# One chunk pipeline before a long loop: ScalarE's evictions run ahead of VectorE's, key rows lag by a row block, one scale for all values, last recalls in four banks

## The chip, the core and the metric

The kernel runs on one NeuronCore of a Trainium2 chip. The number compared is the device time of one execution in microseconds (us). The kernel before the change takes 1706.84 us, the median of 3 runs that lie between 1706.77 and 1707.49 us. The profile is one more execution, taken with the hardware profiler on.

The engines are named as the profile does it: PE (TensorE, with its weight loads as PEld), DVE (VectorE), ACT (ScalarE), POOL (GpSimd) and SP (SyncE, which issues the DMAs). Each engine takes its instructions in the order of its own list, and waits at an instruction until what it needs is there.

## What is computed

The input x has 2048 rows (tokens) of 576 columns. Two results of it are mixed, row by row, with a gate:

```python
g = sigmoid((x * gate_w).sum(-1))
out = g * A(x) + (1 - g) * B(x)
B = (gelu(x @ w_gate) * (x @ w_up)) @ w_down          # hidden width 4608
# A: 32 heads of 18, four chunks of 512 tokens, one after the other
for s in range(4):
    q, k, v = the rows of chunk s of x @ wq, x @ wk, x @ wv
    a_dot = softmax(q k^T * 18**-0.5 + causal mask) @ v
    a_mem = phi(q) M / (phi(q) z + 1e-6)               # "recall"
    o[s]  = sigmoid(beta) * a_mem + (1 - sigmoid(beta)) * a_dot
    M, z  = M + phi(k)^T v, z + sum(phi(k))            # "memorize"
A = o @ wo
phi(t) = t + 1 if t > 0 else exp(t)
```

The weights come in float32. Products with x are made in pairs of fp16 words (a high word and the rest, the low word), scaled by powers of two that are taken from sums of squares.

## The kernel before

The program has three parts. Lines 569 to 761 (the code in the `manual_schedule(engines=ORDERED)` block) project x to queries, keys and values and carry the memory along; this text calls them the opening. Then 72 steps of a loop compute the attention of the 32 heads, for two halves of the tokens, beside the feed-forward B; an end multiplies by wo. Nearly all of the span is the loop, and the change is in the opening and at the loop's first steps.

**The opening's stages.** For a chunk s of 512 tokens there are two stages. In the *rows* of chunk s (s = 1, 2, 3) four row blocks q of 128 tokens follow each other: `vrows(s, q, 0)` and `vrows(s, q, 1)` make the two halves of the value rows (14 matmuls each, in banks `dn`, L312 to L315), `key_rows(s-1, q)` turns the phi of the earlier chunk's keys by five transposes (L531 to L534), `recall` multiplies the phi of its queries with the memory (12 matmuls, L508; from chunk 1 on) and `memorize` adds its keys and values to the memory (L546, banks `U` and `pv`). In the *products* of chunk s come nine chains `project(s, j)` of 14 matmuls of 512 columns (L302 to L305): j = 0 to 4 hold the queries, 4 to 8 the keys. Chain j goes to PSUM bank `G` (j % 4 = 0), `U` (1) or one of two `st`. For chunk 0 the value rows are made first, from float32 words, while the weights arrive, and only the products belong to the stage as said. The recalls of the last chunk come after its chains 5 to 8.

**Evicting a chain** takes: on ACT the high word to the tile `stage` (L449), and where phi is wanted a Relu (L453) and an Exp (L454); on DVE the linear half of phi (L455) and the low word (L457); on POOL the sum of both halves (L456); then a DMA of `stage` to DRAM (L458). `stage` has two buffers. These are written directly behind the chain that they evict.

**Beside the chains.** In the stages of the opening other work is fitted in by `beside_rows` and `beside_products`: pairs of words of the weights (`make_qk`, `make_v`, L103 on ACT and L104 on DVE), the next chunk of x (`next_x`: load, squares, scale, high words on ACT L160, low words on DVE L165), sums of two chunks of x that the feed-forward uses (`load_sums` and `load_rest` L329 and L335, `form_sums`: L349 on DVE, L350 on ACT, L352 on DVE), and in chunk 3 the weights of the first two blocks of the feed-forward (`squares` L80, `scale_g` L252, `sums_g` L272 to L275, `high_g` L279, `low_g` L283). `keep_memory` (L559, L560) moves the memory from PSUM to the tile `bd`, which the next recalls read.

**What sets the order.** In the opening and the loop PE, ACT, DVE and POOL keep the order in which the program is written. SP's order is set by a scheduler, which places each DMA by when it expects the data and the buffer.

## Time and profile before

| what | value |
|---|---|
| median of 3 runs | 1706.84 us |
| the profiled execution | 1714.4 us, its span 1712.7 us |
| mean clock granted to PE | 0.988 |
| PE busy in the span | 1645.0 us (96%) |
| chunk 0's chains to the end of the last chain of chunk 3 (31.72 to 275.48) | 243.76 us |
| the loop and the end (275.48 to 1712.70) | 1437.22 us, PE busy 1406.47 us |

In rows of a timeline the first number is when an instruction (or a row of equal ones, x12) starts, in us from the span's start, and the second how long it takes; then engine, line, operation, output tile <- input tiles, shape. `[1.72 <-DVE stage L457]` behind it says that the engine was idle for 1.72 us before, and that what it waited for ended with VectorE's line 457. Rows of windows give the busy time of each engine in a stretch of the span and the granted clock (1.00 is full).

### The profile page before, as it was taken

To read this page: it belongs to the slowest core of one execution; us is meant where nothing else is said; L and a number is where in the kernel's file an instruction comes from. 1 tells how busy PE (TensorE), PEld (TensorE's weight loads), DVE (VectorE), ACT (ScalarE), POOL (GpSimd) and SP (SyncE) were. 2 spreads that over 40 slices of the span, in tenths; PEclk is the share of its full clock that TensorE was granted. 3 is DMA by queue.
4 is the path that set the end of the run, shared out by engine and by line. 5 is a ranking of instruction groups with operands and counts; after the bars stand their busy time and mean duration, and the time that the engine had idled before them with its cause. 6 is when DMAs were issued, how large, how long until landed. Compare 5 with 4: busy or idle time off the path is not lost.

```text
span 1712.7 us, 31984 instructions
## 1 busy us (share of the span) xinstructions
PE 1645.0 (96%) x11886; PEld 989.7 (58%) x11886; DVE 1267.3 (74%) x3169; ACT 1081.7 (63%) x1768; POOL 1162.8 (68%) x1070
## 2 busy tenths in 40 slices
PE   8899869799999999999999999999999999999999
PEld 4456544355655565555655565555555565565577
DVE  5556566588888878888887778788887888876553
ACT  6565341677777776777677777777777777762200
POOL 3331371888888787888878687978878697876300
PEclk9999888999999999999999999999999999999999
DMA  6532323357565656647465656547465655534441
GB/s 205 200 101 93 112 84 101 72 107 130 109 123 114 126 125 118 128 100 138 102 133 112 134 123 117 124 107 137 107 129 112 141 123 112 120 78 114 92 118 63
DMA packets 462348, 200.54 MB, mean 117 GB/s; under 512 B 421232, under 2 KB 431728, under 8 KB 461680
## 3 DMA queue, kind: packets, MB, share of 16 engines
q1 hardware_dynamic: 462192, 198.50, 52.0%
q8 instruction: 93, 1.52, 0.4%
q14 instruction: 63, 0.52, 0.1%
HBM read 82.60 MB, written 27.26 MB: 64 GB/s over the span
## 4 chain that ended last, share of the span: by engine, by line
PE 67%; DVE 16%; ACT 6%; POOL 6%; issue 3%; DMA 2%; DVEq 0%; ACTq 0%; SPq 0%; POOLq 0%
PE dn L908 17%; PE U L950 13%; PE V L950 7%; PE G L950 7%; PE pv L862 3%; PE st L312 3%; DVE pf L820 3%; PE st L814 2%; DVE acc L916 2%; PE V L957 2%; DVE junk L80 2%; PE dn L312 2%; POOL hh L935 2%; PE U L957 2%; PE G L957 1%
## 5 line engine op out<-in xcount | busy, mean ns | idle before, releaser
L908 PE MATMUL dn<-paird,hh 128*128 128x288 f16 x3402 | 488.6, 286 | 5.1 <-DVE acc L916 4.1
L950 PEld LDWEIGHTS <-pairg 128*128 128x128 f16 x3024 | 290.9, 98 | 300.5 <-issue 30.6
L843 POOL TENSOR_TENSOR ph<-pf,ph 128x512 f16<-128x512 f32 (+1 forms) x256 | 359.1, 1403 | 97.9 <-ACT ph L842 61.0
L908 PEld LDWEIGHTS <-hh 128*128 128x128 f16 x3456 | 337.2, 98 | 144.4 <-issue 8.3
L916 DVE SCALAR_TENSOR_TENSOR acc<-dn,ev,acc 128x288 f32<-128x288 f32 x535 | 268.1, 512 | 51.3 <-PE dn L908 48.9
L833 ACT ACTIVATE pf<-pf,mb,esc 128x512 f32<-128x512 f32 (+3 forms) x512 | 293.0, 642 | 3.0
L935 POOL TENSOR_TENSOR hh<-gl,hh 128x512 f16<-128x512 f32 x144 | 173.0, 1201 | 178.9 <-ACT hh L934 178.9
L820 DVE CUSTOM_DVE_ANT_0 pf<-st,mask 128x512 f32<-128x512 f32 (+3 forms) x512 | 229.2, 485 | 76.0 <-PE st L814 72.8
L950 PE MATMUL U<-xt,pairg 128*128 128x512 f16 x864 | 211.0, 380 | 4.8 <-DVE gl L1064 3.9
L950 PE MATMUL G<-x,pairg 128*128 128x512 f16 x864 | 210.7, 380 | 0.0
L283 POOL TENSOR_TENSOR pairg<-raw,pairg 128x512 f16<-128x512 f32 (+2 forms) x144 | 180.9, 1279 | 13.8 <-ACT pairg L279 13.8
L842 ACT ACTIVATE ph<-pf 128x512 f16<-128x512 f32 (+1 forms) x256 | 184.3, 720 | 0.0
L940 ACT ACTIVATE gl<-gl,sc 128x512 f32<-128x512 f32 x144 | 103.6, 720 | 98.3 <-DVE gl L1081 54.1
L830 ACT ACTIVATE mb<-mx,esc 128x4 f32<-128x4 f32 x128 | 37.3, 292 | 192.2 <-DVE mx L820 192.1
L934 ACT ACTIVATE hh<-gl 128x512 f16<-128x512 f32 x144 | 89.6, 622 | 85.3 <-DVE gl L930 85.3
L252 POOL TENSOR_SCALAR raw<-raw,sc 128x640 f32<-128x640 f32 x72 | 138.8, 1940 | 0.0
L1064 DVE COPY gl<-U 128x512 f32<-128x512 f32 x72 | 49.8, 692 | 108.9 <-POOL hh L935 55.3
L950 PE MATMUL V<-x,pairg 128*128 128x512 f16 x432 | 105.7, 381 | 11.4 <-DVE gl L1049 11.4
L814 PE MATMUL st<-kt,qt 72*128 72x512 f16 (+3 forms) x512 | 111.5, 299 | 0.6 <-DVE mx L820 0.6
L950 PE MATMUL U<-x,pairg 128*128 128x512 f16 x432 | 105.5, 380 | 2.5 <-DVE gl L1081 2.3
L950 PE MATMUL V<-xt,pairg 128*128 128x512 f16 x432 | 105.6, 381 | 1.5 <-DVE mo L522 1.5
L957 PEld LDWEIGHTS <-pairg 128*128 128x128 f16 x576 | 56.6, 98 | 68.6 <-issue 1.1
(247 smaller groups left out, 2590.8 us busy)
## 6 DMA issues: line engine op xcount, KB each, us to landing
raw<-in_wgu_dram SPq DMA_DIRECT2D x36, 640.0 KB
rawd<-in_wd_dram SPq DMA_DIRECT2D x36, 288.0 KB
qk<-stage SPq DMA_DIRECT2D x36, 256.0 KB
qt<-qk SPq DMA_DIRECT2D x128, 72.0 KB
kt<-qk SPq DMA_DIRECT2D x128, 72.0 KB
vp<-vstage SPq DMA_DIRECT2D x16, 296.0 KB
vt<-vp SPq DMA_DIRECT2D x16, 296.0 KB
orow<-oa SPq DMA_DIRECT2D x16, 288.0 KB
```

Source lines behind the costliest of these rows:

```text
L252: pool.tensor_scalar(r, r, scl[f // 2][0][:, 0:1], None, OP.mult)
L283: pool.tensor_tensor(spot(f, *p, 1), raw_g[f][:, p[0] : p[1]], spot(f, *p, 0), OP.subtract)
L814: pe.matmul(o[:, off : off + n], q[:, e * L + qi * P : e * L + (qi + 1) * P], kt[:, e * L : e * L + n], start=True, stop=True)
L820: dve.tensor_tensor_reduce(prob[a][:, COL[qi] : COL[qi + 1]], o[:, off : off + n], mask[:, L - n :], 1.0, -3e38, OP.add, OP.max, mx[a][:, ...
L833: act.activation(r, r, AF.Exp, bias=b[:, qi : qi + 1], scale=esc[:, 0, c : c + 1])
L842: act.activation(h[:, 0, cols], p[:, cols], AF.Copy)
L843: pool.tensor_tensor(h[:, 1, cols], p[:, cols], h[:, 0, cols], OP.subtract)
L908: pe.matmul(o[:, :NH], hh[:, a, q * P : (q + 1) * P], w[:, b, n * NH : (n + 1) * NH], start=i == 0, stop=i == 5)
L916: dve.scalar_tensor_tensor(av, o[:, :NH], ev, av, OP.mult, OP.add)
L935: pool.tensor_tensor(hh[:, 1], t, hh[:, 0], OP.subtract)
L950: pe.matmul(o, w[:, i, (a + k) * P : (a + k + 1) * P], x[:, b + k], start=start and k == 0 and i == 0 and b == h, stop=k == 1 and i == 1, ...
L957: pe.matmul(o, w[:, i, a * P : (a + 1) * P], x[:, b], start=False, stop=i == 1, skip_group_check=True)
```

## The change

1. `project` issues the matmuls alone. ACT's part of an eviction is in `put_columns(j)`, called after the matmuls of chain j+1; what DVE, POOL and SP do for it is put in a list `later` and issued by `finish_later` behind it. `put_rows` and `recall` put VectorE's part in the same list. Bank `U` is that of j % 4 = 3 now, and `key_rows` uses a bank `st` instead of `G`.
2. `key_rows` and `memorize` follow one row block behind the value rows; block 3's key rows come ahead of the chains and its memorize after chain 0. `keep_memory` comes at chain 1.
3. The value weights have one scale instead of one for each half: one `scale_v`, and five `make_v` of 578 columns instead of ten of 288 or 290. Chunk 0's opening is reordered to match.
4. The squares of chunk 1 of x go from POOL to ACT. `form_sums` of the last two chunks is one chain later.
5. In chunk 3 the scaling, sums and words of the feed-forward's block 1 are no longer among the products: they are issued as the loop's other blocks are, in its first steps.
6. The last recalls: blocks 0 and 1 after chain 6 in four banks (`dn`, `dn`, `V`, `pv`), block 2 after chain 7, block 3 at the end.

```diff
...
     def square_x(c, k):
-        r, sq = x_raw[c][k // 2][:, (k % 2) * L : (k % 2 + 1) * L], x_sq[c][:, k * L : (k + 1) * L]
-        if c == 1:
-            pool.tensor_tensor(sq, r, r, OP.mult)
-        else:
-            act.activation(sq, r, AF.Square)
+        act.activation(x_sq[c][:, k * L : (k + 1) * L], x_raw[c][k // 2][:, (k % 2) * L : (k % 2 + 1) * L], AF.Square)
     def scale_x(c):
...
-        def make_v(b, k):
-            if b == 0:
-                W[9 + k] = pa.tile([P, 2, KT * P], F16, name="wv", bufs=5)
-            pair_of(W[9 + k][:, :, VB[b]], raw_v[:, k, VB[b]], wsc[:, 1 + b : 2 + b])
+            square_sum(wst[:, 10 + j : 11 + j], raw_qk[:, j], j % 2 or j == 8)
+        def scale_v():
+            scale_sum(1, wst[:, 0 : 2 * KT])
...
+        def make_v(k):
+            t = W[9 + k] = pa.tile([P, 2, D + 2], F16, name="wv", bufs=5)
+            pair_of(t, raw_v[:, k], wsc[:, 1:2])
...
             pair_of(W[j], raw_qk[:, j], wsc[:, 0:1])
+        later = []
+        def finish_later():
+            while later:
+                later.pop(0)()
         def project(s, j):
-            hf, c = divmod(s, 2)
             w = W[j]
             i = j % 4
-            pr = bank("G") if i == 0 else bank("U") if i == 1 else bank("st", 2)
+            pr = bank("G") if i == 0 else bank("U") if i == 3 else bank("st", 2)
             chain_w(pr, lambda k, a: w[:, a, k * P : (k + 1) * P], x16[s])
+            return s, j, pr
+        def put_columns(s, j, pr):
+            hf, c = divmod(s, 2)
             st = pp.tile([P, 2, L], F16, name="stage", bufs=2)
             act.activation(st[:, 0], pr, AF.Copy, scale=2.0**-14)
-            if (j <= 4 and s >= 1) or (j >= 4 and s <= 2):
+            with_phi = (j <= 4 and s >= 1) or (j >= 4 and s <= 2)
+            if with_phi:
...
                 act.activation(e, e, AF.Exp, scale=-1.0)
-                dve.tensor_scalar(f, pr, al[:, s, 0:1], 0.0, OP.mult, OP.max)
-                pool.tensor_tensor(f, f, e, OP.add)
-            dve.scalar_tensor_tensor(st[:, 1], pr, 2.0**-14, st[:, 0], OP.mult, OP.subtract)
-            sp.dma_start(qks[hf][:, j * P : (j + 1) * P, c * L : (c + 1) * L].rearrange("a p t -> p a t"), st)
+            def rest():
+                if with_phi:
+                    dve.tensor_scalar(f, pr, al[:, s, 0:1], 0.0, OP.mult, OP.max)
+                    pool.tensor_tensor(f, f, e, OP.add)
+                dve.scalar_tensor_tensor(st[:, 1], pr, 2.0**-14, st[:, 0], OP.mult, OP.subtract)
+                sp.dma_start(qks[hf][:, j * P : (j + 1) * P, c * L : (c + 1) * L].rearrange("a p t -> p a t"), st)
+            later.append(rest)
         def put_rows(s, q, b, pv, unit, a):
...
-            put_rows(s, q, b, pv, 2.0**-14, al[:, s, 1 + b : 2 + b])
+            return pv, 2.0**-14, al[:, s, 1:2]
         def first_words(pvs, b, k, qs):
...
-            hf, c = divmod(s, 2)
-            t = 4 * c + q
-            na, nb = (spare(), spare()) if s == 3 else (bank("st", 2), bank("st", 2))
+        def recall(s, q, banks=(("st", 2), ("st", 2))):
...
                               start=first, stop=last, skip_group_check=True)
+            later.append(lambda: put_recall(s, q, na, nb))
...
         def key_rows(s, q):
-            ka, kb = bank("G"), bank("V")
+            ka, kb = bank("st", 2), bank("V")
...
-                if j == 1 + d:
-                    for k in range(3 + 2 * d):
+                if j in (2, 3):
+                    for k in ((0, 1, 2), (3, 4))[j - 2]:
                         square_x(c, k)
...
-                if j == 4 + d:
+                if j == 4:
                     scale_x(c)
...
                 if s == 2:
+                    if q:
+                        form_sums(0, q - 1, 1)
...
                     if q == 1:
-                        squares(0, 0, 0)
-                        squares(0, 0, 1)
+                        for f, i in ((0, 0), (0, 1), (1, 0), (1, 1)):
+                            squares(0, f, i)
                     if q == 2:
-                        squares(0, 1, 0)
-                        squares(0, 1, 1)
...
             def beside_products(s, j):
-                if s < 3:
-                    next_x(s + 1, j)
...
                         make_qk(j + 2)
-                    for i in ((0, 1), (2, 3, 4), (5, 6, 7), (8, 9))[j] if j < 4 else ():
-                        make_v(i // KT, i % KT)
+                    if j < 5:
+                        make_v(j)
+                if s < 3:
+                    next_x(s + 1, j)
                 if s == 2:
+                    if j == 0:
+                        form_sums(0, 3, 1)
+                        last_sum(0, 0)
+                    if j == 1:
+                        last_sum(0, 1)
...
                 if s == 3:
-                    if j in (0, 3):
-                        high_g(j // 3, 0)
-                        low_g(j // 3, 0)
-                        sums_g(j // 3)
-                    if j in (1, 4):
-                        high_g(j // 3, 1)
-                        low_g(j // 3, 1)
+                    if j == 0:
+                        high_g(0, 0)
+                        low_g(0, 0)
+                    if j == 1:
+                        sums_g(0)
                     if j == 2:
+                        high_g(0, 1)
+                    if j == 3:
+                        low_g(0, 1)
+                    if j == 4:
                         load_g(3)
-                        scale_g(1)
+                    if 3 <= j < 7:
+                        form_sums(1, j - 3, 1)
                     if 2 <= j < 6:
-                        form_sums(1, j - 2, 1)
-                    if 1 <= j < 5:
-                        form_sums(1, j - 1, 0)
-                    if j in (5, 6):
-                        squares(1, 2, j - 5)
-                    if j == 6:
+                        form_sums(1, j - 2, 0)
+                    if j in (6, 7):
+                        squares(1, 2, j - 6)
+                    if j == 7:
                         last_sum(1, 0)
+            done = None
...
                     for q in range(4):
-                        vrows(s, q, 0)
-                        key_rows(p, q)
+                        pv = vrows(s, q, 0)
+                        if done:
+                            put_columns(*done)
+                            done = None
+                        finish_later()
+                        put_rows(s, q, 0, *pv)
+                        if q:
+                            key_rows(p, q - 1)
+                        beside_rows(s, q)
+                        finish_later()
                         if p >= 1:
                             recall(p, q)
-                        beside_rows(s, q)
-                        vrows(s, q, 1)
-                        memorize(p, q)
-                        if s == 2:
-                            form_sums(0, q, 1)
-                    if s == 2:
-                        last_sum(0, 0)
-                        last_sum(0, 1)
-                    keep_memory(p)
-                make_gate(s)
...
                 for j in range(9):
+                    if j == 1:
+                        make_gate(s)
+                    pr = project(s, j)
+                    if s and j == 0:
+                        memorize(p, 3)
+                    if done:
+                        put_columns(*done)
+                    done = pr
+                    if s and j == 1:
+                        keep_memory(p)
+                    if s == 3 and j == 1:
...
-                    project(s, j)
-                    if s == 3 and j >= 5:
-                        recall(3, j - 5)
+                    finish_later()
+                    if s == 3 and j == 6:
+                        recall(3, 0, (("dn", 2), ("dn", 2)))
+                        recall(3, 1, (("V",), ("pv",)))
+                    if s == 3 and j == 7:
+                        recall(3, 2, (("dn", 2), ("dn", 2)))
+            recall(3, 3)
+            put_columns(*done)
+            finish_later()
...
         def weights_first(fb, i4):
             n0 = 2 * fb
-            if not fb and i4 < 2:
-                return
...
             if i4 == 1:
...
         def weights_high(fb, i4):
             n0 = 2 * fb
-            if fb or i4 >= 2:
-                high_g(n0 + 1 + i4 // 2, i4 % 2)
+            high_g(n0 + 1 + i4 // 2, i4 % 2)
...
             n0 = 2 * fb
-            if fb or i4 >= 2:
-                low_g(n0 + 1 + i4 // 2, i4 % 2)
+            low_g(n0 + 1 + i4 // 2, i4 % 2)
             if i4 >= 2:
                 low_d(n0 + i4 - 2)
```

What the lists of the engines look like where the prediction speaks of them:

ScalarE, the first products of chunk 3, before: `stage` and `expm` evict a chain, `xt` is the high word of a sum of two chunks, `raw` to `pairg` a weight's high word.

```order
L449 ACTIVATE stage<-G 128x512
L453 ACTIVATE expm<-G,nal 128x512
L454 ACTIVATE expm<-expm 128x512
L279 ACTIVATE pairg<-raw 128x512 x2
L350 ACTIVATE xt_2101<-acc,xsc 128x1024
L449 ACTIVATE stage<-U 128x512
L453 ACTIVATE expm<-U,nal 128x512
L454 ACTIVATE expm<-expm 128x512
L350 ACTIVATE xt_2101<-acc,xsc 128x1024
L449 ACTIVATE stage<-st 128x512
L453 ACTIVATE expm<-st,nal 128x512
L454 ACTIVATE expm<-expm 128x512
```

And now:

```order
L453 ACTIVATE stage<-G 128x512
L458 ACTIVATE expm<-G,nal 128x512
L459 ACTIVATE expm<-expm 128x512
L453 ACTIVATE stage<-st 128x512
L458 ACTIVATE expm<-st,nal 128x512
L459 ACTIVATE expm<-expm 128x512
L274 ACTIVATE pairg<-raw 128x512 x2
L345 ACTIVATE xt_2112<-acc,xsc 128x1024
L453 ACTIVATE stage<-st 128x512
L458 ACTIVATE expm<-st,nal 128x512
L459 ACTIVATE expm<-expm 128x512
L345 ACTIVATE xt_2112<-acc,xsc 128x1024
```

Two chains are evicted ahead of the first `xt` now instead of one, and the third eviction stands behind one `xt`, where it stood behind two.

VectorE at the same place, before (`acc` is a sum of two chunks, `xt` with three operands its low word):

```order
L349 TENSOR_TENSOR acc<-acc 128x1024
L455 TENSOR_SCALAR phi<-U,al 128x512
L457 SCALAR_TENSOR_TENSOR stage<-U,stage 128x512
L352 SCALAR_TENSOR_TENSOR xt_2101<-acc,xsc,xt_2101 128x1024
L349 TENSOR_TENSOR acc<-acc 128x1024
L455 TENSOR_SCALAR phi<-st,al 128x512
L457 SCALAR_TENSOR_TENSOR stage<-st,stage 128x512
L352 SCALAR_TENSOR_TENSOR xt_2101<-acc,xsc,xt_2101 128x1024
L349 TENSOR_TENSOR acc<-acc 128x1024
L455 TENSOR_SCALAR phi<-st,al 128x512
```

And now:

```order
L344 TENSOR_TENSOR acc<-acc 128x1024
L463 TENSOR_SCALAR phi<-st,al 128x512
L465 SCALAR_TENSOR_TENSOR stage<-st,stage 128x512
L347 SCALAR_TENSOR_TENSOR xt_2112<-acc,xsc,xt_2112 128x1024
L344 TENSOR_TENSOR acc<-acc 128x1024
L463 TENSOR_SCALAR phi<-st,al 128x512
L465 SCALAR_TENSOR_TENSOR stage<-st,stage 128x512
L347 SCALAR_TENSOR_TENSOR xt_2112<-acc,xsc,xt_2112 128x1024
L344 TENSOR_TENSOR acc<-acc 128x1024
L463 TENSOR_SCALAR phi<-U,al 128x512
```

VectorE's list is the same there but for the banks: `U` is the fourth chain's now.

SyncE in the products of chunk 0, before: `qk` is the store of an evicted chain, `acc` a load of the chunks of x that are summed later (2048 words for each partition, 1 MB; `2x512`, half of that).

```order
L458 DMA qk<-stage 128x2x512
L329 DMA acc<-in_xs_dram 128x2048
L458 DMA qk<-stage 128x2x512
L335 DMA acc<-in_xs_dram 128x2x512
L458 DMA qk<-stage 128x2x512
L329 DMA acc<-in_xs_dram 128x2048
L458 DMA qk<-stage 128x2x512
L329 DMA acc<-in_xs_dram 128x2048
L458 DMA qk<-stage 128x2x512 x2
L329 DMA acc<-in_xs_dram 128x2048
L458 DMA qk<-stage 128x2x512
```

And now:

```order
L324 DMA acc<-in_xs_dram 128x2048
L466 DMA qk<-stage 128x2x512
L330 DMA acc<-in_xs_dram 128x2x512
L466 DMA qk<-stage 128x2x512 x2
L324 DMA acc<-in_xs_dram 128x2048
L466 DMA qk<-stage 128x2x512
L324 DMA acc<-in_xs_dram 128x2048
L466 DMA qk<-stage 128x2x512
L324 DMA acc<-in_xs_dram 128x2048
L466 DMA qk<-stage 128x2x512
```

The loads of x's sums stood behind the first, second, third, fourth and sixth store; now they stand ahead of the first, second, fourth, fifth and sixth.

More of the change, by code (lines that the diff above doesn't have):

```diff
@@ L114, in outscale @@
         else:
[L115 to L116 removed]
+            pool.tensor_scalar(gha[:, c], gh[:, 1], al[:, c, o], 2.0**14, OP.mult, OP.mult)
     x_raw = {}
@@ L475, in put_rows, with rest @@
                 act.activation(v32[s, q][:, hs, 0:DH], p3, AF.Copy, scale=a)
-            dve.scalar_tensor_tensor(st[:, hs, DH : 2 * DH], p3, unit, st[:, hs, 0:DH], OP.mult, OP.subtract)
-            if b:
-                dve.tensor_scalar(gate[:, 0, 8 * hf + t : 8 * hf + t + 1], pv[:, NH : NH + 1], a, None, OP.mult)
-                sp.dma_start(vps[hf][t * P : (t + 1) * P, :], flat(st))
+            def rest():
+                dve.scalar_tensor_tensor(st[:, hs, DH : 2 * DH], p3, unit, st[:, hs, 0:DH], OP.mult, OP.subtract)
+                if b:
+                    dve.tensor_scalar(gate[:, 0, 8 * hf + t : 8 * hf + t + 1], pv[:, NH : NH + 1], a, None, OP.mult)
+                    sp.dma_start(vps[hf][t * P : (t + 1) * P, :], flat(st))
+            later.append(rest)
         def vrows(s, q, b):
@@ L493, in first_words @@
                           start=k == 0, stop=k == 4)
-        def recall(s, q):
-            hf, c = divmod(s, 2)
-            t = 4 * c + q
-            na, nb = (spare(), spare()) if s == 3 else (bank("st", 2), bank("st", 2))
+        def recall(s, q, banks=(("st", 2), ("st", 2))):
+            na, nb = (bank(*i) for i in banks)
             for j, (a, w) in enumerate(SPANS):
@@ L582 @@
             va = [bank("dn", 2), bank("dn", 2), bank("V"), bank("pv")]
-            for k in range(3):
+            for k in range(2):
                 first_words(va, 0, k, range(4))
@@ L1139, in finish @@
                     wos[k] = op_.tile([P, 2, D], F16, name="wo", bufs=5)
-                    pair_of(wos[k], rows[k], wsc[:, 3:4])
+                    pair_of(wos[k], rows[k], wsc[:, 2:3])
         LAG = 2
```

109 lines of the change are left out of this document (51 added, 58 removed).

## The prediction

> **What bounds the kernel now.** I read the strip of 40 slices first, for where PE is not full.
>
> ```profile
> PE   8899869799999999999999999999999999999999
> ```
>
> After slice 7 (some 300 us) PE is full to the end, so what the change can win lies ahead of that. The next view is the table of windows, cut at the stages of the opening: the products of chunk 0, then rows and products of chunks 1, 2 and 3.
>
> ```profile
> core 0: us, PE busy (x) PEld busy (x) DVE busy (x) ACT busy (x) POOL busy (x), PEclk, DMA share, GB/s
> 31.72:65.43 33.71, 29.42 (x131) 12.32 (x132) 27.32 (x48) 21.90 (x41) 14.25 (x15) 1.00 0.70 226
> 65.43:93.82 28.39, 24.66 (x173) 18.34 (x171) 11.00 (x23) 12.22 (x30) 7.64 (x18) 0.94 0.36 128
> 93.82:122.11 28.29, 28.29 (x134) 12.81 (x132) 16.86 (x33) 19.71 (x33) 12.71 (x15) 1.00 0.31 99
> 122.11:153.53 31.42, 29.65 (x221) 23.73 (x220) 19.43 (x44) 13.80 (x30) 6.40 (x12) 1.00 0.29 103
> 153.53:182.74 29.21, 28.44 (x133) 12.80 (x132) 20.41 (x38) 21.52 (x36) 12.70 (x15) 1.00 0.37 118
> 182.74:222.75 40.01, 34.83 (x224) 27.33 (x222) 18.66 (x59) 8.08 (x21) 8.21 (x13) 0.87 0.26 96
> 222.75:275.48 52.73, 37.89 (x175) 19.75 (x175) 37.01 (x61) 21.90 (x34) 34.08 (x24) 0.84 0.31 106
> ```
>
> The products of chunk 1 are the measure: nine chains and a norm's sum in 28.29 us, PE busy all of it at clock 1.00. Chunk 3 runs as much work and its four recalls, and takes 40.01 + 52.73 = 92.74 us at clocks 0.87 and 0.84. PE's timeline prices the work at full clock and shows the waits.
>
> ```profile
> 126.64 1.76 PE L508 MATMUL st<-bd,phi 128*128 128x152 f32 x12
> 133.99 1.76 PE L508 MATMUL st<-bd,phi 128*128 128x152 f32 x12
> 264.51 2.76 PE L302 MATMUL st<-x,wp 128*128 128x512 f16 x12
> 267.54 1.76 PE L508 MATMUL dn<-bd,phi 128*128 128x152 f32 x12
> 186.34 0.24 PE L531 MATMUL G<-ident,phi 64*128 64x64 f32 x1 [1.72 <-DVE stage L457]
> 187.25 3.05 PE L508 MATMUL st<-bd,phi 128*128 128x152 f32 x12
> 210.38 0.36 PE L85 MATMUL dn<-stat,ones 128*128 128x8 f32 x2 [3.43 <-DVE stat L80]
> 251.94 0.88 PE L508 MATMUL dn<-bd,phi 128*128 128x152 f32 x2 [8.89 <-POOL phi L456]
> 256.52 0.70 PE L508 MATMUL dn<-bd,phi 64*128 64x76 f32 x2 [3.71 <-POOL phi L456]
> 275.48 2.08 PE L950 MATMUL V<-xt,pairg 128*128 128x512 f16 x6 [1.46 <-DVE mo L522]
> ```
>
> From recall to recall a row block of chunk 2 takes 133.99 - 126.64 = 7.35 us; a chain takes 267.54 - 264.51 = 3.03 us; a recall 1.7. Chunk 3 at these prices: 4 x 7.35 + 0.2 (a small sum) + 9 x 3.03 + 4 x 1.7 = 63.7 us. It loses 92.74 - 63.7 = 29 us. The waits quoted at 186.34, 210.38, 251.94 and 256.52 are 17.8 us of it (the last row's, 1.46, comes after the cut); most of the rest, some 11 us, is work at a low clock behind them: the recall at 187.25 takes 3.05 us where that at 126.64 takes 1.76.
>
> **Why the recall waits 8.89 us.** It wants phi of chains 2 to 4, and these come late on DVE:
>
> ```profile
> 239.81 0.75 DVE L455 TENSOR_SCALAR phi<-st,al 128x512 f32<-128x512 f32 x1 [2.28 <-ACT expm L453]
> 241.07 2.30 DVE L352 SCALAR_TENSOR_TENSOR xt<-acc,xsc,xt 128x1024 f16<-128x1024 f32 x1
> 243.30 2.41 DVE L349 TENSOR_TENSOR acc<-acc 128x1024 f32<-128x1024 f32 x1
> 247.99 0.75 DVE L455 TENSOR_SCALAR phi<-st,al 128x512 f32<-128x512 f32 x1 [2.28 <-ACT expm L453]
> 245.74 1.15 ACT L350 ACTIVATE xt<-acc,xsc 128x1024 f16<-128x1024 f32 x1 [4.12 <-DVE acc L349]
> ```
>
> It is a ring of two engines. ACT's high word at 245.74 has waited 4.12 us for DVE's sum; the eviction of the next chain stands behind it in ACT's list, and DVE then waits 2.28 us for that eviction. One turn takes 247.99 - 239.81 = 8.18 us where a chain takes 3.03, so PE has made the chains long before.
>
> **The change, stage by stage** (gains +, in us of the profiled execution).
>
> *Chunk 3.* The lists show that ACT now evicts a chain ahead of the `xt` that waits for DVE's sum; DVE's list stays as it was. So DVE no longer waits for ACT and its own work sets phi. PE is through chain 6 at 7 x 3.03 + 1.3 (memorize: 0.78 + 0.53 in the last two rows here, of the chain of waits) = 22.5 us from the start of the chains; then the first recall wants phi of chain 4. DVE begins with `keep_memory`, which now waits for memorize behind chain 0, to 4.3 us:
>
> ```profile
> 222.50 0.62 DVE L559 TENSOR_TENSOR krow<-U,bdm 128x456 f32<-128x456 f32 x1
> 226.01 0.15 DVE L565 TENSOR_SCALAR gate<-gate 128x4 f32<-128x4 f32 x1
> 130.00 1.21 DVE L349 TENSOR_TENSOR acc<-acc 128x1024 f32<-128x1024 f32 x1
> 133.62 1.28 DVE L352 SCALAR_TENSOR_TENSOR xt<-acc,xsc,xt 128x1024 f16<-128x1024 f32 x1
> 255.21 1.26 POOL L456 TENSOR_TENSOR phi<-phi,expm 128x512 f32<-128x512 f32 x1 [0.65 <-DVE phi L455]
> 235.29 5.77 POOL L252 TENSOR_SCALAR raw<-raw,sc 128x640 f32<-128x640 f32 x2
> 81.29 0.78 PE U L546 x6
> 82.06 0.53 PE pv L546 x4
> ```
>
> That takes 226.01 - 222.50 = 3.5, to 7.8. Behind it: four evictions of 241.07 - 239.81 = 1.26, three low words, three full sums and a half one, then phi of chain 4 (0.75) and POOL's sum (1.26). At chunk 2's 1.21 and 1.28 these sums are 3 x 1.28 + 3.5 x 1.21 = 8.1, and phi is there at 7.8 + 5.0 + 8.1 + 0.75 + 1.26 = 22.9: PE waits 0.4. At the 2.30 and 2.41 of chunk 3 they are 15.3 and phi is there at 30.1: PE waits 8. The long ones lie beside POOL's scaling (5.77 at 235.29) and low words of block 1, and those are moved out of this place, so I take a value nearer the short end, 3. A second wait I put at 2: recall 2 takes the banks of recall 0, whose eviction stands behind two squares and an eviction on DVE. The waits at 186.34 (`key_rows` one block later), 210.38 (squares a block earlier) and the other recalls' go. Chunk 3 loses 5 instead of 29: **+24**, from +18 (8 and 2, and 1 of low clock) to +28.5.
>
> [...]
>
> *Rows and products of chunk 2.* Row and chain prices give 57.7 us where 60.63 are used. `[1.74 <-DVE stage L457]` ahead of the first transposes goes as in chunk 3, for the first phi wanted is now a half row block later:
>
> ```profile
> 125.73 0.24 PE L531 MATMUL G<-ident,phi 64*128 64x64 f32 x1 [1.74 <-DVE stage L457]
> ```
>
> With the memory's move at the other end (PE is idle 0.8 in the products) that is **+2.5**, from 0 to 2.9.
>
> [...] The trace shows both: behind 1.72 at 186.34 the recall took 3.05, behind 1.74 at 125.73 it took 1.76. [...]
>
> *Products of chunk 0, rows of chunk 1.* They take 62.1 us; at full clock some 28.3 + 4 x 5.65 = 50.9 (the row block of chunk 2 less a recall), so 11 are lost. DVE (27.32 busy of 33.71) and the stores of `stage` set it:
>
> ```profile
> 49.69 0.35 SPq L329 DMA_DIRECT2D acc<-in_xs_dram  x1
> 50.29 7.87 DMA qk<-stage
> 64.36 4.40 DMA qk<-stage
> 58.27 0.60 ACT L449 ACTIVATE stage<-U 128x512 f16<-128x512 f32 x1 [3.85 <-DMA qk<-stage]
> ```
>
> A store issued behind a 1 MB load lands after 7.87 us, a later one after 4.40, and ACT, with two buffers, waits for them. What helps: five conversions of the value weights instead of ten, and POOL's squares off DVE's way. What hurts: SP's new list puts a 1 MB load ahead of the stores of chains 3, 4 and 5, the store itself comes one chain later, and behind ACT's wait stand the conversion of the last key weight and chunk 1's x, so the rows of chunk 1 start late. Two buffers give two chains for each landing + 3.3 us (an estimate: a high word of 0.6, and the low word about a chain behind it): 5.6 us a chain at 7.87 for three or four chains, against 3.03. I put the loss at 13 instead of 11: **-2**, from -6 to +5 (no store beyond 4.40).
>
> *The start of the chains.* PE waits 0.55 there for the first query weight, whose scale now comes one row block earlier:
>
> ```profile
> 31.72 0.61 PE L302 MATMUL G<-x,wp 128*128 128x512 f16 x2 [0.55 <-ACT wp L103]
> ```
>
> **+0.5**, from 0. One scale for all values lets the first evictions wait for the second half's squares too; they lie ahead of nothing that PE waits for until its banks come round.
>
> *The loop's first steps* get block 1's scaling, sums and words, some 12 us of POOL by an estimate (the scaling's 5.77, and as much again for low words and sums). They fit into POOL's idle time:
>
> ```profile
> 288.52 1.16 POOL L935 TENSOR_TENSOR hh<-gl,hh 128x512 f16<-128x512 f32 x1 [29.30 <-ACT hh L934]
> ```
>
> so they cost nothing, or up to 4 if POOL's list holds `hh` back. The loop starts without the wait of 1.46 at most and warm: **+0.7**, from -4 to +1.5. Products of chunk 1 are full already: 0.
>
> **Sum:** 24 + 2.5 - 2 + 0.5 + 0.7 = 25.7. The profiled execution would take 1714.4 - 25.7 = 1688.7. It stands 7.6 above the median; I carry the difference over in microseconds: 1706.84 - 25.7 = 1681.1, **1681**.
>
> **Rivals.**
> - *All waits go and PE is the bound of the whole opening*: 28.5 + 2.9 + 5 + 0.5 + 0.7 = 37.6, 1669. For it: PE's work is the same; against it: even undisturbed, phi comes at 22.9 against 22.5, and chunk 0 keeps its loads. 0.15.
> - *DVE is the bound in chunk 3*, its instructions as long beside POOL's as at 241.07: waits of 8 for phi and 2 for banks, squares as long as the one below, low clock behind them: a loss of 16 there instead of 29, +13, 14.7 in all, 1692. For it: POOL keeps block 0's words and four phi sums there. 0.17.
>
> ```profile
> 257.05 2.86 DVE L80 CUSTOM_DVE_ANT_0 junk<-raw 128x640 bf16<-128x640 f32 x1
> ```
>
> - *Slower: the stores of chunk 0 become the bound.* Each waits behind a load, two buffers, (landing + 3.3) / 2 us a chain. The other terms give +27.7, so it decides from 33.7 + 27.7 = 61.4 us for the nine chains, 6.8 each, a landing of 10.3 us. At 12 us: 9 x 7.65 = 69, a loss of 35, 1714. Against it: the longest landing is 7.87, and only five stores have a load ahead. 0.05.
> - *The waits only move* (the clock stays low in chunk 3 with shorter waits spread over it, and chunk 0 loses more): under 3 us, 1705. That ACT does not run ahead would show the same. The lists speak against both. 0.05.
>
> **Chances.** The forecast has 0.58. About 0.2% (3.4 us) is what a measurement of this kernel can tell from no change. Faster by more: 0.58 + 0.15 + 0.17 = 0.90; the same 0.05; slower 0.05. The forecast's own range is 1675 to 1687; to hold eight in ten it goes on to most of both faster rivals: 1671 to 1695.
>
> **What would show it.** In windows cut at the stages: chunk 3 at 68 to 72 us with a clock above 0.95, chunk 2 at 58, chunks 0 to 1 at 60 to 66 with ACT waiting for `qk<-stage` before the evictions of chains 5 and later. The waits of DVE for `expm` are gone; the first recall of chunk 3 waits for POOL's phi by 0 to 5 us. It is wrong if PE waits 8 or more there, if `hh` in the loop's first steps comes later, or if a store lands after 10 us.

## The result and the profile after

The changed kernel takes 1690.15 us (median of 4 runs, 1689.41 to 1691.98) where the kernel before takes 1707.16 us (median of 4): 0.9899 of it, with a 95% interval of 0.9882 to 0.9916. That is 17.0 us less, 14 to 20 by the interval. The forecast was 25.7 us less, 1681, with a range of 1671 to 1695. Ratios are of undisturbed executions; one execution, the profiled one of the last experiment, took 7800 us and is left out with its profile. Lines of the changed kernel are numbered a few higher or lower than before: a chain is L297 to L300, value rows L307 to L310, `key_rows` L548 to L551, recall L520, `put_columns` L453 to L459 on ScalarE and L463, L465 on VectorE, the sum of phi L464, a row's low word L488.

The windows of the changed kernel, cut at the same stages as those of before (products of chunk 0, then rows and products of chunks 1, 2 and 3, then all that follows):

```profile
core 0: us, PE busy (x) PEld busy (x) DVE busy (x) ACT busy (x) POOL busy (x), PEclk, DMA share, GB/s
31.18:60.98 29.80, 28.77 (x132) 12.60 (x132) 19.02 (x36) 19.82 (x33) 4.38 (x9) 1.00 0.73 249
60.98:89.44 28.46, 23.83 (x163) 17.46 (x162) 12.88 (x25) 14.05 (x32) 5.43 (x12) 0.88 0.39 137
89.44:119.13 29.69, 29.69 (x143) 14.10 (x141) 16.20 (x29) 20.06 (x35) 11.25 (x13) 1.00 0.29 93
119.13:149.27 30.14, 28.27 (x212) 22.79 (x210) 24.10 (x49) 14.04 (x30) 6.89 (x11) 1.00 0.31 112
149.27:178.96 29.69, 29.69 (x144) 14.10 (x141) 17.72 (x33) 19.98 (x34) 10.23 (x13) 1.00 0.32 105
178.96:213.78 34.82, 30.19 (x214) 23.45 (x213) 21.18 (x61) 8.45 (x20) 12.42 (x15) 0.95 0.35 121
213.78:254.70 40.92, 38.81 (x186) 21.44 (x184) 33.93 (x55) 19.91 (x32) 19.29 (x14) 0.92 0.33 111
254.70:1690.30 1435.60, 1404.94 (x10615) 845.37 (x10614) 1103.83 (x2818) 947.77 (x1512) 1067.25 (x936) 1.00 0.55 115
```

Set beside the windows of before, in us (the last memorize of a chunk, 1.4 us, now stands behind its first chain, and so in the products):

| place | before | after | gain | forecast |
|---|---|---|---|---|
| up to the first chain | 31.72 | 31.18 | 0.5 | 0.5 |
| products of chunk 0, rows of chunk 1 | 62.10 | 58.26 | 3.8 | -2 |
| products of chunk 1 | 28.29 | 29.69 | -1.4 | 0 |
| rows and products of chunk 2 | 60.63 | 59.83 | 0.8 | 2.5 |
| rows and products of chunk 3 | 92.74 | 75.74 | 17.0 | 24 |
| loop and end | 1437.22 | 1435.60 | 1.6 | 0.7 |
| span | 1712.7 | 1690.3 | 22.4 | 25.7 |

The profiles show 22.4, the medians 17.0. The first experiment takes up that difference.

Chunk 3 lost 29 us before and loses 75.74 - 63.7 = 12 now, not 5. PE's timeline shows what is left:

```profile
70.53 2.92 PE L307 MATMUL dn<-wv,x 128*128 128x288 f16 x12 [2.07 <-DVE vstage L488]
126.31 1.63 PE L307 MATMUL dn<-wv,x 128*128 128x288 f16 x12 [1.87 <-DVE vstage L488]
189.06 2.90 PE L307 MATMUL dn<-wv,x 128*128 128x288 f16 x12 [4.62 <-DVE vstage L488]
239.84 0.44 PE L520 MATMUL dn<-bd,phi 64*128 64x76 f32 x2 [2.11 <-POOL phi L464]
243.33 4.69 PE L297 MATMUL U<-x,wp 128*128 128x512 f16 x12
```

The wait for phi is 2.11 us where it was 8.89 and 3.71. But three waits are new: in each of chunks 1, 2 and 3 the first value rows of row block 1 wait for their bank `dn`, 2.07, 1.87 and 4.62 us. They take the place of PE's waits ahead of the first transposes (1.66, 1.74 and 1.72 before), half a row block later, and the last is longer. What the last one waits for is on ScalarE's and VectorE's timelines:

```profile
183.43 0.60 ACT L453 ACTIVATE stage<-G 128x512 f16<-128x512 f32 x1 [3.08 <-DMA qk<-stage]
185.17 0.71 ACT L483 ACTIVATE vstage<-dn 128x288 f16<-128x288 f32 x2
186.21 2.26 DVE L170 TENSOR_SCALAR x<-x,xr 128x4608 f16<-128x4608 f16 x1
188.57 0.44 DVE L488 SCALAR_TENSOR_TENSOR vstage<-dn,vstage 128x288 f16<-128x288 f32 x1
```

ScalarE waits 3.08 us for a store of `stage` before it can evict chain 8, and does so 4.47 us after the rows began (183.43 - 178.96), where it was 0.89 before (183.63 - 182.74). Behind that stands the value rows' high word, then on VectorE the rescale of x (2.26 us), and only then the low word that frees the bank.

The ring is gone as forecast. VectorE's phi of a chain follows that of the chain before in 4.3 us, where a turn took 8.18, and it no longer waits for ScalarE:

```profile
229.52 0.74 DVE L463 TENSOR_SCALAR phi<-st,al 128x512 f32<-128x512 f32 x1
233.84 0.74 DVE L463 TENSOR_SCALAR phi<-U,al 128x512 f32<-128x512 f32 x1
```

### The profile page after: what moved, and what is told of

It reads as the page before. It is cut to its first block, busy times and chain, and to the rows that moved or that the text cites. A ratio compares the mean times of both kernels' runs of the same rounds, so it can differ in the third digit from the quotient of the medians.

```text
span 1690.3 us, 31950 instructions
## 1 busy us (share of the span) xinstructions
PE 1638.8 (97%) x11884; PEld 987.6 (58%) x11884; DVE 1266.0 (75%) x3154; ACT 1083.6 (64%) x1770; POOL 1146.5 (68%) x1057
## 4 chain that ended last, share of the span: by engine, by line
PE 68%; DVE 16%; ACT 7%; POOL 4%; issue 3%; DMA 2%; DVEq 0%; ACTq 0%; SPq 0%; POOLq 0%
PE dn L942 17%; PE U L984 13%; PE V L984 7%; PE G L984 7%; PE pv L896 3%; DVE pf L854 3%; PE st L307 3%; PE st L848 3%; PE V L991 2%; DVE acc L950 2%; DVE junk L80 2%; PE dn L307 2%; PE U L991 2%; DMA qk<-stage 1%; POOL hh L969 1%
## 5 line engine op out<-in xcount | busy, mean ns | idle before, releaser
L984 PEld LDWEIGHTS <-pairg 128*128 128x128 f16 x3024 | 290.6, 98 | 298.2 <-issue 27.6
L80 DVE CUSTOM_DVE_ANT_0 junk<-raw 128x640 bf16<-128x640 f32 x72 | 96.5, 1340 | 0.1
```

Source lines behind the costliest of these rows:

```text
L80: dve.tensor_tensor_reduce(junk[:, : r.shape[1]], r, r, 1.0, 1e-30, OP.mult, OP.add, o)
L984: pe.matmul(o, w[:, i, (a + k) * P : (a + k + 1) * P], x[:, b + k], start=start and k == 0 and i == 0 and b == h, stop=k == 1 and i == 1, ...
```

## The experiments

Three questions were open: how much of the profiles' 22.4 us is the change, what holds the three new waits, and which part of the change carries the gain in chunk 3. Ratios are to the kernel before on the same chip; runs that were made on one chip are named together. The changed kernel itself has 0.9899 and, in a second measurement, 0.9877, so 0.9888 is taken where a variant was measured on another chip; one thousandth is 1.7 us.

### Both kernels again, three buffers, rows first (one chip)

**The kernel before once more.** Nothing is changed.

> The kernel before, unchanged, for a second profiled execution. The first was 7.6 us above its median, that of the change 1.8 above its own. If the excess is the hardware's choice of clock in that one execution, chunk 3 takes some 86 to 88 us here instead of 92.74, at a higher granted clock; if a profile of this kernel always has it, chunk 3 takes 92 to 93 again.

This profiled execution took 1709.19 us instead of 1714.4. The windows from the rows of chunk 3 on:

```profile
183.21:221.03 37.82, 32.79 (x224) 25.82 (x222) 18.63 (x59) 8.07 (x21) 8.27 (x13) 0.91 0.28 101
221.03:273.98 52.95, 38.12 (x176) 19.93 (x175) 37.05 (x61) 21.89 (x34) 34.08 (x24) 0.84 0.31 105
273.98:1707.50 1433.52, 1401.95 (x10614) 844.48 (x10614) 1101.65 (x2814) 945.29 (x1507) 1058.81 (x928) 1.00 0.56 114
```

Chunk 3 takes 90.77 us, 2 less than in the first profile and above the 86 to 88 expected; the products are the same within 0.2. The loop takes 3.7 us less. So of the 5.2 us between the two profiled executions 3.7 lie in the loop; whether both ran on the same chip is not on record. Against this second profile the changed kernel's opening gains 273.98 - 254.70 = 19.3 us and its loop loses 2.1, together 17.2, close to the medians' 17.0. The loop alone differed by 3.7 us between two executions of one program; a difference of stages between single profiles cannot be read finer than that.

**The changed kernel once more.** Nothing is changed.

> The changed kernel, unchanged, timed on the same chip as the next two: 0.990 of before, by either theory; its profile shows the waits of 2.07, 1.87 and 4.62 us ahead of row block 1 again.

1690.97 us, 0.9877 (0.9862 to 0.9892). The waits ahead of row block 1 are 2.15, 2.07 and 4.55 us: as before, and in the same places.

**Three buffers for `stage`.**

```diff
-            st = pp.tile([P, 2, L], F16, name="stage", bufs=2)
+            st = pp.tile([P, 2, L], F16, name="stage", bufs=3)
```

> The tile stage gets three buffers instead of two; nothing else. Theory A, the waits ahead of row block 1 come from the stores: ScalarE's eviction of chain 8 waits for the store of chain 6, and the value rows' eviction stands behind it. Then ScalarE's waits for the stores go, the rows of chunk 3 take 30 to 31 us instead of 34.8 and the start of chunk 1's rows gains 3 or more: 6 to 10 us less than the changed kernel. Theory B, VectorE's own list sets it (rescale of 2.26 us and chain 8's phi ahead of the row's low word): 0 to 2 us less.

1676.79 us, 0.9794 (0.9780 to 0.9809): 14.2 us less than the changed kernel on this chip, more than the 6 to 10 expected. Windows of the rows of chunks 1, 2 and 3 and of the products of chunk 3, then the one wait of ScalarE for a store that is left in the whole opening (the changed kernel has ten):

```profile
60.63:82.90 22.27, 21.41 (x163) 16.60 (x162) 9.95 (x23) 9.86 (x25) 4.58 (x11) 1.00 0.38 129
112.59:140.70 28.11, 28.11 (x211) 22.80 (x210) 23.67 (x48) 13.90 (x29) 6.92 (x11) 1.00 0.32 114
170.40:199.37 28.97, 28.42 (x213) 22.95 (x212) 19.41 (x59) 7.23 (x17) 11.42 (x14) 1.00 0.37 132
199.37:238.64 39.27, 37.15 (x187) 20.28 (x184) 33.64 (x55) 19.81 (x32) 19.30 (x14) 0.96 0.31 105
62.03 0.60 ACT L453 ACTIVATE stage<-G 128x512 f16<-128x512 f32 x1 [2.13 <-DMA qk<-stage]
```

The rows of chunk 1 fall from 28.46 to 22.27 us, those of chunk 2 from 30.14 to 28.11, those of chunk 3 from 34.82 to 28.97, and their clock is 1.00. Theory A holds: the stores, with two buffers, made the new waits. The order in which SyncE issues stores and loads at the start of chunk 3's rows is the same in both kernels, so a load moved out of the way is not the reason there. VectorE's list is the same, rescale included, and costs PE 0.55 us there; theory B is out. Whether a third buffer would also have helped the kernel before, where ScalarE waits five times for a store (1.88 to 3.85 us), was not tried.

**Rows first.** In a row stage `put_rows(s, q, 0, *pv)` is called ahead of `put_columns(*done)`.

```diff
+                        put_rows(s, q, 0, *pv)
                         if done:
                             put_columns(*done)
                             done = None
                         finish_later()
-                        put_rows(s, q, 0, *pv)
```

> In a row stage the eviction of the first value half is issued ahead of that of chain 8, on ScalarE and VectorE; two buffers as before. Both theories put the wait ahead of row block 1 down to what stands in front of the row's low word, so both expect it gone: 5 to 9 us less than the changed kernel. A rival: the store still holds ScalarE at chain 8, now in front of the second half's eviction, and the wait moves on by one half without getting shorter: 0 to 2 us less.

1689.07 us, 0.9858 (0.9840 to 0.9877). That is 1.9 us less than the changed kernel, and the intervals overlap. In chunk 3 PE goes on past the bank and then waits, row block 1's transposes for a bank `st` of the recall:

```profile
182.41 0.60 ACT L453 ACTIVATE stage<-G 128x512 f16<-128x512 f32 x1 [1.95 <-DMA qk<-stage]
188.30 0.82 DVE L539 TENSOR_TENSOR mo<-st,rden 128x288 f32<-128x288 f32 x2
188.91 0.34 PE L548 MATMUL st<-ident,phi 64*128 64x64 f32 x1 [3.77 <-DVE mo L539]
```

The rival was right: the wait moved on by half a row block and kept most of its length (3.77 for 4.62; PE also waits 1.03 for the last words of x a little earlier). Reordering does not help while the list as a whole is late by a store.

### One part undone at a time (one chip)

**No deferral.** Each chain is evicted straight behind its own matmuls.

```diff
-                    if done:
-                        put_columns(*done)
-                    done = pr
+                    put_columns(*pr)
+                    finish_later()
...
             recall(3, 3)
-            put_columns(*done)
             finish_later()
```

> The changed kernel with each chain evicted on ScalarE, VectorE and POOL directly behind its own matmuls and ahead of the work beside it, as before; all else as changed. Theory A (the ring of ScalarE and VectorE was what held phi): the eviction is still ahead of that chain's sums here, so ScalarE does not stand behind the sum that VectorE has not made; the ring need not come back, and the time is within 3 us of the changed kernel, better at the chunk boundaries since the stores start one chain earlier. Theory B (the deferral itself is what wins): waits of 6 to 9 us for phi come back ahead of the first recall of chunk 3, 8 to 14 us more than the changed kernel.

1699.99 us, 0.9935 (0.9914 to 0.9956), 8 us more than the changed kernel. I had argued in theory A that the ring need not come back. It does:

```profile
236.40 0.75 DVE L463 TENSOR_SCALAR phi<-U,al 128x512 f32<-128x512 f32 x1 [3.38 <-ACT expm L458]
244.04 0.75 DVE L463 TENSOR_SCALAR phi<-G,al 128x512 f32<-128x512 f32 x1 [2.28 <-ACT expm L458]
246.28 0.70 PE L520 MATMUL dn<-bd,phi 64*128 64x76 f32 x2 [4.39 <-POOL phi L464]
257.63 2.23 PE L520 MATMUL dn<-bd,phi 128*128 128x152 f32 x12 [3.36 <-DVE mo L539]
```

VectorE waits the same 2.28 us for ScalarE's Exp as before the change, and a turn takes 7.64 us. The high word of a sum again stands in front of the next chain's eviction; that a chain's eviction is ahead of its *own* sums changes nothing. So the deferral breaks the ring, as theory B has it, though PE waits 4.39 us for phi and 3.36 for recall 0's late eviction, and not 6 to 9 at once.

**No lag.** `key_rows(p, q)` and `memorize(p, q)` at row block q; the extra calls behind the rows and behind chain 0 are dropped.

```diff
-                        if q:
-                            key_rows(p, q - 1)
+                        key_rows(p, q)
...
-                        if q:
-                            memorize(p, q - 1)
+                        memorize(p, q)
```

> key_rows and memorize at their own row block again, all else as changed. Theory A (PE's wait at a chunk boundary is for ScalarE's eviction of chain 8, held by a store): the transposes of row block 0 want phi of chain 8 at once, so PE waits there for it, in place of the wait for the value rows' bank a half block later: 1 to 6 us more. Theory B (the lag is worth nothing because the bank's wait takes its place): 0 to 1 us of difference.

1702.30 us, 0.9948 (0.9933 to 0.9963), 10 us more than the changed kernel, and more than expected. The transposes of row block 0 wait for phi of chain 8, in chunk 2 (the first row) and in chunk 3:

```profile
127.89 0.48 PE L551 MATMUL V<-ident,phi 128*128 128x128 f32 x1 [2.74 <-POOL phi L464]
194.89 0.47 PE L551 MATMUL V<-ident,phi 128*128 128x128 f32 x1 [3.69 <-POOL phi L464]
195.16 3.22 PE L520 MATMUL st<-bd,phi 128*128 128x152 f32 x12
```

With evictions deferred, phi of chain 8 comes later than it did before the change (where PE waited 1.74 and 1.72), so the deferral needs the lag. Behind the wait the recall runs at the low clock (3.22 us for 1.76), which I had left out of the expectation.

**Block 1 back.** The feed-forward's block 1 is scaled, summed and split among chunk 3's chains 2 to 4 again, and the loop's first steps leave it out.

```diff
+                    if j == 2:
+                        load_g(3)
+                        scale_g(1)
+                    if j == 3:
+                        high_g(1, 0)
+                        low_g(1, 0)
+                        sums_g(1)
                     if j == 4:
-                        load_g(3)
+                        high_g(1, 1)
+                        low_g(1, 1)
...
```

> The scaling, sums and words of the feed-forward's block 1 are put back among chunk 3's chains 2 to 4; the loop's first steps leave them out again; all else as changed. Theory A (POOL's long instructions beside VectorE's sums stretch them): the sums take 2.0 to 2.4 us again where some take 1.2, POOL's phi stands behind them, and the wait ahead of the first recall of chunk 3 is 6 to 9 us instead of 2.1: 5 to 9 us more. Theory B (the ring alone made it): the wait stays at 2 to 3, 0 to 2 us of difference.

1699.13 us, 0.9934 (0.9912 to 0.9956), 8 us more than the changed kernel. PE waits 4.66 and 3.68 us in the first recall, together 8.3, the size that theory A gave. Its reason is not the one that theory A named:

```profile
238.01 0.63 ACT L274 ACTIVATE pairg<-raw 128x512 f16<-128x512 f32 x1 [5.97 <-POOL raw L268]
241.33 1.68 DVE L347 SCALAR_TENSOR_TENSOR xt<-acc,xsc,xt 128x1024 f16<-128x1024 f32 x1 [5.82 <-ACT xt L345]
240.87 1.20 PE L520 MATMUL dn<-bd,phi 128*128 128x38 f32 x4 [4.66 <-POOL phi L464]
245.74 0.62 PE L520 MATMUL dn<-bd,phi 128*128 128x152 f32 x1 [3.68 <-POOL phi L464]
```

ScalarE waits 5.97 us for POOL's sums of block 1 before a high word of the weights, and VectorE 5.82 us for the `xt` behind it. It is a longer ring, through POOL. The stretched sums are the smaller part: the full ones take 1.20 to 2.17 us with block 1 there and 1.20 to 2.17 without.

**Recalls back.** Behind chains 5 to 8, in turns in `dn`, `dn` and `V`, `pv`.

```diff
-                    if s == 3 and j == 6:
-                        recall(3, 0, (("dn", 2), ("dn", 2)))
-                        recall(3, 1, (("V",), ("pv",)))
-                    if s == 3 and j == 7:
-                        recall(3, 2, (("dn", 2), ("dn", 2)))
-            recall(3, 3)
+                    if s == 3 and j >= 5:
+                        recall(3, j - 5, (("dn", 2), ("dn", 2)) if j % 2 else (("V",), ("pv",)))
```

> The last recalls stand behind chains 5 to 8 again, in turns in the banks dn and dn, V and pv; all else as changed. By the sum that holds in the changed kernel phi of chain 4 is complete 2.1 us after PE is through chain 6; a chain earlier PE would wait 2.1 + 3.0 = 5 us and then run at a low clock: 3 to 6 us more. A rival: what PE waits there it saves at the end, where recall and evictions stand behind the last chain: 0 to 1 us of difference.

1695.28 us, 0.9910 (0.9892 to 0.9928), 3.8 us more than the mean of the changed kernel's two ratios; but the intervals overlap, so this cost is not shown by the times.

```profile
236.90 0.53 PE L520 MATMUL dn<-bd,phi 128*128 128x152 f32 x2 [1.64 <-POOL phi L464]
240.67 0.70 PE L520 MATMUL dn<-bd,phi 64*128 64x76 f32 x2 [3.25 <-POOL phi L464]
258.92 1.46 PE L980 MATMUL V<-xt,pairg 128*128 128x512 f16 x6 [1.46 <-DVE mo L539]
```

PE waits 1.64 + 3.25 = 4.9 us in the first recall, by the sum 2.1 + 3.0 = 5, and the wait of 1.46 at the loop's start is back. The loop starts 4.2 us later than in the changed kernel.

### One part alone, one part undone, and the last wait (one chip)

**Before, with block 1 out.** In the kernel before, the calls for block 1 leave chunk 3's products and go to the loop's first steps; nothing else.

```diff
-                    if j in (0, 3):
-                        high_g(j // 3, 0)
-                        low_g(j // 3, 0)
-                        sums_g(j // 3)
-                    if j in (1, 4):
-                        high_g(j // 3, 1)
-                        low_g(j // 3, 1)
+                    if j == 0:
+                        high_g(0, 0)
+                        low_g(0, 0)
+                        sums_g(0)
+                    if j == 1:
+                        high_g(0, 1)
+                        low_g(0, 1)
                     if j == 2:
                         load_g(3)
-                        scale_g(1)
...
```

> The kernel before with one part of the change alone: block 1's scaling, sums and words go from chunk 3's chains to the loop's first steps. Theory A (the ring of ScalarE and VectorE holds phi by itself): a turn of the ring is still a high word, an eviction, a low word and a sum, 0.58 + 0.68 + 0.63 on ScalarE in turn with VectorE's work; the sums fall from 2.3 to 1.2 us, a turn from 8.2 to some 6, and the wait of 8.89 us to 2 to 4: 6 to 9 us less than before. Theory B (the parts only work together): 0 to 3 us less.

1706.89 us, 0.9979 (0.9963 to 0.9995), by the ratio 3.6 us less than before, between the two theories.

```profile
237.31 0.75 DVE L455 TENSOR_SCALAR phi<-st,al 128x512 f32<-128x512 f32 x1 [2.28 <-ACT expm L453]
243.99 0.75 DVE L455 TENSOR_SCALAR phi<-st,al 128x512 f32<-128x512 f32 x1 [2.28 <-ACT expm L453]
246.22 0.87 PE L508 MATMUL dn<-bd,phi 128*128 128x152 f32 x2 [5.98 <-POOL phi L456]
251.94 0.70 PE L508 MATMUL dn<-bd,phi 64*128 64x76 f32 x2 [4.84 <-POOL phi L456]
```

The ring turns in 6.68 us instead of 8.18, as theory A had it, but VectorE's 2.28 us stay and the waits are 5.98 + 4.84 where they were 8.89 + 3.71: less than 2 us shorter. Alone, taking out block 1 is worth 3.6 us; with the other parts in place it is worth 8. The parts need each other: undone one at a time, the deferral, the lag and block 1's move cost 8, 10 and 8 us, 26 together, where the whole change gains some 19. The deferral in the kernel before, without the rest, was not tried.

**Chunk 1's squares back on POOL.** `square_x` as before.

> The changed kernel with the squares of chunk 1 of x on POOL again. Theory A (chunk 0's gain, 3.8 us in its chains where a loss of 2 was forecast, comes from VectorE, which no longer stands beside POOL's squares): VectorE's words of the weights take longer again, and chunk 0's chains take 2 to 4 us more. Theory B (it comes from the halved number of conversions alone): 0 to 1 us of difference.

1692.10 us, 0.9885 (0.9858 to 0.9912): no difference. That part of the change is worth nothing that can be measured here; chunk 0's chains take 30.57 us (31.21 to 61.78) where the changed kernel's take 29.80 and those before the change 33.71, so most of what they gained does not come from it. Whether it comes from the five conversions in place of ten was not tried.

**Sums one chain later.**

```diff
-                    if 3 <= j < 7:
-                        form_sums(1, j - 3, 1)
-                    if 2 <= j < 6:
-                        form_sums(1, j - 2, 0)
+                    if 4 <= j < 8:
+                        form_sums(1, j - 4, 1)
+                    if 3 <= j < 7:
+                        form_sums(1, j - 3, 0)
```

> The changed kernel with the sums of the last two chunks of x one chain later in chunk 3, so that one sum and one low word less stand ahead of phi of chain 4 on VectorE: 0.68 + 1.96 = 2.6 us. Theory A (VectorE's list sets the wait of 2.1 us ahead of the first recall, and the low clock behind it): the wait goes, and with it the chain of 4.69 us instead of 2.76: 3 to 5 us less than the changed kernel. Theory B (the low clock comes from something else, or the loop now waits for the late sums): 0 to 2 us less, or more time.

1692.43 us, 0.9891 (0.9872 to 0.9910): no difference. The wait of 2.11 us in the first recall is gone, as theory A expected. It came back as another. The first of these lines is from the changed kernel, the others from this run:

```profile
245.95 0.82 DVE L539 TENSOR_TENSOR mo<-dn,rden 128x288 f32<-128x288 f32 x2
239.80 2.83 DVE L344 TENSOR_TENSOR acc<-acc 128x512 f32<-128x512 f32 x1
238.75 3.33 POOL L352 TENSOR_TENSOR acc<-acc 128x1024 f32<-128x1024 f32 x1
246.99 0.82 DVE L539 TENSOR_TENSOR mo<-dn,rden 128x288 f32<-128x288 f32 x2
247.60 2.00 PE L520 MATMUL dn<-bd,phi 128*128 128x152 f32 x12 [3.39 <-DVE mo L539]
249.53 4.23 PE L297 MATMUL G<-x,wp 128*128 128x512 f16 x12
```

Recall 2 needs the banks of recall 0, and VectorE evicts these (`mo`) 9.61 us after PE began recall 0, in this run (246.99 - 237.38) as in the changed kernel (245.95 - 236.34): what moved still stands in front of it. In the changed kernel the first wait (2.11 us) and the low clock behind it (4.69 us for a chain of 2.75) keep PE from recall 2 until 248.29; here PE is there early, waits 3.39 us, and the next chain runs at the low clock (4.23 us). VectorE is busy for 33.93 of the 40.92 us of this stage in the changed kernel, and a shift by one chain does not free it.

**Three buffers and the later sums.** Both edits.

> Three buffers for stage and the later sums together. If both waits are what they seem, the gains add: three buffers gave 0.9794 of before, the later sums 3 to 5 us more, so 0.976 to 0.978. If PE's low clock in chunk 3 has another cause, no better than 0.979.

1679.10 us, 0.9814 (0.9792 to 0.9837): not better than three buffers alone. The gains do not add, because the second is none.

So the fastest version is the changed kernel with three buffers for `stage`, 0.9794 of before; the later sums add nothing to it.

## Why the prediction was right and where it was not

- **The ring.** Right. The stall for phi came from ScalarE standing behind a sum that VectorE had not made, and letting ScalarE run ahead removed it; without the deferral VectorE's 2.28 us are there again. It was not enough alone: with block 1 left among the chains a longer ring, through POOL, forms in spite of the deferral.
- **Phi of chain 4 at 22.9 to 30.1 us, PE's wait put at 3.** Right in size: phi was there at 26.0 us (238.52 + 1.26 - 213.78), and PE, which had begun the recall at 22.6, waited 2.11. My reason for the choice was partly wrong. The long sums were put down to POOL's scaling of block 1; without it four of seven still take 1.96 to 2.17 us, beside block 0's low words and POOL's sums of phi.
- **The second wait, put at 2.** It did not show: the low clock behind the first wait (4.69 us for a chain of 2.75), some 3.3 us of the 5.4 that the products lost (5.4 - 2.11, an estimate), which the sum had left out, brought PE to recall 2 too late to wait. The later sums laid it bare, 3.39. That 5.4 came so near to the 5 forecast is luck.
- **Block 1 moved at no cost in the loop.** No cost is seen: 1435.60 us for the loop, between the 1433.52 and 1437.22 of before's two profiles.
- **"The waits at 186.34, 210.38 and the other recalls' go. Chunk 3 loses 5 instead of 29."** This step failed: it loses 12, of which 6.6 lie in the rows (34.82 less 4 x 7.35 + 0.2 - 1.4, the last for the memorize that moved), where nothing was forecast, and 5.4 in the products. The wait at 210.38 went. That at 186.34 was replaced by the bank's, 4.62 us, with a low clock behind it (2.90 for 1.63). I had named the mechanism, ScalarE held by two `stage` buffers, but priced it for chunk 0 only. At the start of chunks 2 and 3 the same lists meet: chain 8's eviction stands now among the rows, about a chain later, and the value rows' low word stands behind it, and behind a sum of two chunks of x (2.00 us) in chunk 2 and the rescale in chunk 3. Three buffers take 5.85 us off the rows of chunk 3, most of what was missing.
- **Chunk 2, +2.5.** It was 0.8; the same bank's wait of 1.87 stands where 1.74 went.
- **Chunk 0 and rows of chunk 1, -2.** The other way: 62.10 to 58.26, of which 1.4 are memorize moved out, so +2.4. What brought that gain is open; moving the squares off POOL did not. The stores landed after 4.75, 2.78 and 4.50 us in the chain of waits, not 7.87, and ScalarE's waits for them (five, 0.97 to 2.51 us) cost PE 0.32 us in the chains and some 4.6 at the start of the rows. The price of a store behind a load was taken from the longest landing.
- **The profile against the median.** I carried the profile's difference over in microseconds. Some 5 us of the profiles' 22.4 are that first execution of before; the opening's own gain is 19 to 21.
- **The total.** That the profiles came as near as 22.4 to 25.7 is luck in part: the 7 us that chunk 3 fell short, and 1.7 in chunk 2, stand against 4.4 that chunk 0 and chunk 1's rows did better.
- **Rivals.** "VectorE is the bound, 1692" is closer in time than the forecast. Its long squares (2.88) and its low clock (0.92 in chunk 3's products) came, but PE's wait for phi was 2.11, not 8, and the 6.6 us in chunk 3's rows are not in it. The stores as a bound in chunk 0 did not come about; as waits, mostly at the start of the rows of chunks 1 to 3, they cost 14 us, by the third buffer.

## What to carry to other kernels

When a deferred eviction needs a buffer longer, look at how many buffers it has in every place where the deferral applies, and above all where two stages meet and a second kind of eviction queues behind the first: here a third buffer was worth 14 us, beside some 19 for the whole change. A wait that ends on one engine's line may be held by an engine or a store two steps back, so follow it to the first idle engine before choosing a remedy; reordering the list in between moved the wait by half a block and kept most of it (3.77 us for 4.62). Where an engine is busy for most of a stage, as VectorE was here for 33.93 of 40.92 us, shifting its work by one step can trade one wait for the next (2.11 for 3.39 us).

## What the runs showed of the hardware

**VectorE beside POOL.** In three places of these runs an instruction of VectorE that starts while one of POOL's runs is longer than elsewhere by about what POOL's has left: by 0.68 us for 0.87, 2.07 for 2.20 and 2.15 for 2.28. Two are from the changed kernel (the squares are `CUSTOM_DVE_ANT_0`):

```profile
230.43 1.26 POOL L464 TENSOR_TENSOR phi<-phi,expm 128x512 f32<-128x512 f32 x1 [1.91 <-DVE phi L463]
230.82 1.96 DVE L347 SCALAR_TENSOR_TENSOR xt<-acc,xsc,xt 128x1024 f16<-128x1024 f32 x1
239.74 2.81 POOL L352 TENSOR_TENSOR acc<-acc 128x1024 f32<-128x1024 f32 x1
240.35 2.88 DVE L80 CUSTOM_DVE_ANT_0 junk<-raw 128x640 bf16<-128x640 f32 x1
```

POOL has 0.87 us left at 230.82, and the low word takes 1.96 for 1.28; it has 2.20 left at 240.35, and the squares take 2.88 for 0.81 (243.77). The third is the half sum of the later-sums run (2.83 at 239.80 for 0.68, with 2.28 left of POOL's). In other places VectorE's instruction kept its length: its sum at 221.74 took 1.20 us, and there the two sums of phi on POOL that span it took 3.92 for 2 x 1.26; in the kernel before, the sum at 236.32, beside POOL's scaling, took 1.21. Why the one or the other is longer was not shown.

**Short waits and the clock.** Behind 1.87 us of waiting the value rows took 1.63 us (granted clock 1.00 from 126.30 to 128.00), behind 2.07 in chunk 1 2.92 (0.55 from 70.50 to 73.50), behind 2.11 the next chain took 4.69 for 2.75 (0.59 from 243.30 to 248.20). In the changed kernel's second profile the wait of 2.07, now in chunk 2, was followed by 1.63. So a wait of some 2 us cost up to as much again in some places and nothing in others. Ahead of the 2.07 in chunk 1 stood waits of 0.60 and 1.96 us, and the value rows between took 2.36 us for 1.64 (0.67 from 65.30 to 68.40), so the clock was low there before that wait. What decides it was not shown; the measured rows give the price in this kernel.
